# A fused attention and feed-forward kernel: the hand-kept order of all five queues and of the PSUM banks is replaced by another

## The chip, the cores and the metric

The kernel runs on one core of a Trainium2 chip. The metric is the device time of one execution in microseconds (us); lower is better. The core has a matrix engine (TensorE; PE in the profile, its weight loads PEld), a vector engine (VectorE, DVE), a scalar engine (ScalarE, ACT), a general engine (GpSimd, POOL) and a queue that only issues transfers (SyncE, SP). Each runs its instructions in the order in which the program lists them, and waits at an instruction until the semaphores that it names are reached.

## The reference

```python
P = sort_net                                  # 4 batches x 8 heads x 8 x 8
for _ in range(5):                            # "Sinkhorn": normalize rows, then columns
    P = exp(P - max(P, -1)); P = P / (sum(P, -1) + 1e-9); P = P / (sum(P, -2) + 1e-9)
k_sorted = einsum('bhij,bhjcd->bhicd', P, k in 8 blocks of 96 rows)    # the same for v
scores = (q_block @ k_sorted_block.T) / 8     # block by block: 96 x 96
attn = softmax(scores);  o = attn @ v_sorted_block
x = o as 3072 tokens x 512                    # batch x sequence, heads side by side
h = x @ w_in                                  # 512 -> 2048
g = max(h, 0) + alpha * min(h, 0)
out = g @ w_out                               # 2048 -> 512
```

q, k and v are 4 x 8 x 768 x 64 and the result 3072 x 512, all float32; the kernel multiplies in bf16.

## The kernel before, in words

The 4 batches of 8 blocks make 32 steps, g = 0 to 31 (batch b = g // 8). A step handles one block of 96 tokens for all 8 heads. What stands here with a line number is line 1 to 1141 of the kernel before; the changed file is one line shorter from the ORDER table on, so that its lines are lower by one.

**Sinkhorn** (lines 546 to 560) is one chain of small instructions on DVE, with one exponential of ACT in each of its five rounds; its last product is `Pb`. PE spreads `Pb` over the partitions (line 570 for batch 0, lines 593 and 597 for the others), and DVE makes the mixing matrices of it: `BDQ` for the keys of batch 0, `BDM` for those of the others, `BDV` for the values.

**Preparation of a batch.** `k` and `v` are loaded by POOL's queue into `KS` and `VST` (two buffers each). For batches 1 to 3 `conv_k` (L659, POOL) and `conv_v` (copies by L399, on POOL, ACT or DVE) lay them out with zeros between; `prep_k` (L671) and `prep_v` (L700) are PE's products with the mixing matrices, and ACT or DVE copies the results to `KT` and `VS`. `q` of batch 0 is transposed by PE (`prep_q`, L631). For the other batches it goes into `QN`, one load for each of 8 heads (L432), and `turn_q` (L442) turns it from `QN` into `QT` by six transposing DMAs on SP, each of which waits for all eight heads.

**A step of attention.** Scores on PE (L740 for batch 0, L737 for the others), the maxima on DVE (L747), the exponential on ACT (L791, L779), the product with `VS` on PE (L802), reciprocal and scaling to `xq` on DVE (L807, L810), and the transposed result in `xT`. In batch 0 the exponential is made on transposed scores, which PE computes a second time (L759) and from which it subtracts the maxima (L771). In the others the exponentials `Esb` are transposed to `ET` by a DMA on SP (L784). `xq` becomes `xT` by PE (L824) and a copy in batches 0 and 1, by a transposing DMA (L817) in batches 2 and 3.

**Feed-forward.** `ffn1` (L845) multiplies `xT` by `w_in` in pieces of 192 or 384 tokens, ACT takes the relu of the negative into `t` (L852), DVE makes `hT` (L856). The first six tiles of 128 tokens are multiplied by `w_out` in the plain way (`ffn2`, L879). The rest goes in pairs, with seven products in place of eight (`ffn2_pair`, products at L939); their sums and differences (L932, and L904 for the weights) run on DVE or POOL, the results are copied or added into `outstg` (L399, L950) and stored by SP (L890, L981).

**What sets the order.** The code above records 1268 operations and what each reads and writes. Two tables then decide all: `ORDER` lists for each of the five queues which operation comes after which (so it also decides whether ACT or DVE, or DVE or POOL, does an operation that either can do), and `BANKS` gives each product its PSUM bank of the eight. An entry with a dot in PE's list, `24.0`, is not an operation but so many idle products of the identity by itself into that bank (L1101). The code derives the semaphores and waits from these tables:

```python
                if e == "pe" and op.ten is not None and op.ten.ops[0] is op:
                    starts.append(op.ten)
...
        for t in starts:
            for b in t.b:
                if holds[b] is not None:
                    t.ops[0].deps.update(x.idx for x in holds[b].ops)
                holds[b] = t
```

## Time and profile before

| | |
|---|---|
| median of 3 runs | 233.16 us (230.76, 233.16 and 234.16) |
| the profiled execution | 231.25 us, its span 229.5 us |
| outside the span | 1.75 us |
| busy in the span | PE 218.8, PEld 158.2, DVE 188.2, ACT 155.0, POOL 143.0 us |
| moved | 29.01 MB, 126 GB/s |

The span runs from the first instruction of the profiled execution to the last. Matrix products overlap each other, and the profile models their ends, so a busy PE says that work is in flight, not that it runs at its peak. Rows of a timeline give the start in the span, the duration, engine, line, operation and tiles; in brackets stands the idle time of the engine ahead of it and what ended it. Times below are those of the profiled execution, counted from the start of its span.

### The profile page before, as it was taken

What the parts mean: (1) busy time and instruction counts of PE and PEld (TensorE: products, weight loads), DVE (VectorE), ACT (ScalarE), POOL (GpSimd) and SP (SyncE); (2) the same over time, 40 slices, a digit from 0 to 9 for tenths busy, and PEclk for the clock granted to TensorE, in tenths of its full rate; (3) what the DMA queues carried; (4) which work ended last, traced back from release to release, by engine and by line L of the source; (5) the groups of instructions that cost most, each with busy time, mean ns of one, the idle gap of its engine ahead of it and who ended that gap; (6) DMA issues with size and microseconds to landing.
All of it is one profiled execution on the core that took longest, in us unless ns stands there. A gap on an engine that the chain in (4) does not pass through costs nothing.

```text
span 229.5 us, 6469 instructions
## 1 busy us (share of the span) xinstructions
PE 218.8 (95%) x2581; PEld 158.2 (69%) x2581; DVE 188.2 (82%) x393; ACT 155.0 (68%) x428; POOL 143.0 (62%) x159
## 2 busy tenths in 40 slices
PE   2989989899999999999999999999999999999995
PEld 2367868787556655756568786787767777666884
DVE  4757899996879978998999988988799977758942
ACT  4335876867898877898887898679876424456220
POOL 7992929669598999999999499437000312095030
PEclk9999999999999999999999999999999999999999
DMA  5999999999769999989995462765624404200115
GB/s 88 192 208 192 212 206 200 197 109 164 143 113 109 227 141 131 152 159 199 138 93 98 86 160 64 99 146 65 148 60 106 97 20 97 85 27 0 72 68 183
DMA packets 64718, 29.01 MB, mean 126 GB/s; under 512 B 55328, under 2 KB 60464, under 8 KB 64688
## 3 DMA queue, kind: packets, MB, share of 16 engines
q0 software_dynamic: 25216, 13.63, 46.6%
q1 hardware_dynamic: 39472, 14.97, 34.3%
q8 instruction: 20, 0.33, 0.6%
q14 instruction: 10, 0.08, 0.1%
HBM read 27.28 MB, written 6.29 MB: 146 GB/s over the span
## 4 chain that ended last, share of the span: by engine, by line
PE 80%; DVE 13%; ACT 3%; POOL 2%; issue 1%; POOLq 0%
PE ps L845 31%; PE ps L939 23%; PE ps L879 9%; PE ps L700 4%; DVE hT L856 3%; PE ps L802 3%; PE ps L737 3%; DVE xq L810 2%; PE ps L671 2%; DVE nm L747 2%; DVE VDz L399 1%; ACT t L852 1%; PE ps L824 1%; DVE SS L932 1%; PE ps L1101 1%
## 5 line engine op out<-in xcount | busy, mean ns | idle before, releaser
L845 PE MATMUL ps<-xT,w_in_bf 128*128 128x384 bf16 (+1 forms) x576 | 96.2, 308 | 0.1
L856 DVE SCALAR_TENSOR_TENSOR hT<-t,omaT,ps 128x384 bf16<-128x384 f32 (+1 forms) x144 | 75.4, 561 | 11.6 <-ACT t L852 11.1
L852 ACT ACTIVATE t<-ps 128x384 f32<-128x384 f32 x128 | 59.1, 494 | 32.1 <-PE ps L845 19.7
L845 PEld LDWEIGHTS ps<-xT,w_in_bf 128*128 128x128 bf16 x576 | 51.0, 98 | 24.7 <-DVE hT L856 0.8
L779 ACT ACTIVATE Esb<-ps,nf 96x96 bf16<-96x96 f32 x192 | 46.2, 354 | 3.2 <-DVE nf L747 3.1
L399 POOL COPY VDz<-VST 64x384 bf16<-64x384 bf16 x40 | 35.0, 875 | 12.4 <-PE ps L700 5.6
L939 PE MATMUL ps<-w_out_bf,hT 128*128 128x256 bf16 x288 | 35.6, 273 | 0.0
L939 PEld LDWEIGHTS ps<-w_out_bf,hT 128*128 128x128 bf16 x288 | 27.6, 98 | 4.2
L659 POOL COPY KSz<-KS 64x512 bf16<-64x512 bf16 x36 | 23.4, 651 | 8.8 <-DMA KS<-in_k_dram 3.9
L747 DVE TENSOR_REDUCE nf<-ps 96x8 f32<-96x768 f32 x24 | 22.6, 949 | 3.9 <-PE ps L737 3.8
L879 PE MATMUL ps<-w_out_bf,hT 128*128 128x512 bf16 x96 | 24.0, 379 | 0.0
L932 POOL TENSOR_TENSOR hT<-hT,SS 128x1024 bf16<-128x1024 bf16 x6 | 12.7, 2124 | 18.1 <-PE ps L939 16.5
L810 DVE TENSOR_TENSOR xq<-ps,rec 96x512 bf16<-96x512 f32 x32 | 21.9, 684 | 0.9
L399 ACT ACTIVATE outstg<-ps 128x256 f32<-128x256 f32 (+1 forms) x28 | 11.6, 419 | 15.1 <-PE ps L939 13.3
L432 POOL DMA_DIRECT2D QN<-in_q_dram x24 | 19.9, 845 | 0.5 <-DMA QT<-QN 0.5
L399 ACT ACTIVATE VS<-ps 112x512 bf16<-112x512 f32 (+1 forms) x24 | 16.3, 689 | 5.2 <-PE ps L700 5.0
L939 PE MATMUL ps<-TS,SS 128*128 128x256 bf16 x144 | 18.5, 272 | 0.5 <-DVE SS L932 0.5
L932 POOL TENSOR_TENSOR SS<-SS,hT 128x1024 bf16<-128x1024 bf16 x3 | 6.4, 2123 | 20.0 <-DVE SS L932 19.9
L932 POOL TENSOR_TENSOR SS<-hT 128x1024 bf16<-128x1024 bf16 x3 | 6.4, 2122 | 16.6 <-DVE hT L856 16.6
L950 DVE TENSOR_TENSOR outstg<-outstg,ps 128x256 f32<-128x256 f32 x27 | 11.1, 413 | 6.8 <-PE ps L939 5.1
L939 PEld LDWEIGHTS ps<-TS,SS 128*128 128x128 bf16 x144 | 13.8, 98 | 3.1 <-issue 0.8
L802 PEld LDWEIGHTS ps<-VS,ET 112*128 112x128 bf16 (+1 forms) x256 | 11.5, 98 | 3.2 <-DVE VS L399 0.6
(113 smaller groups left out, 290.3 us busy)
## 6 DMA issues: line engine op xcount, KB each, us to landing
out_dram<-outstg SPq DMA_DIRECT2D x22, 256.0 KB, 2.5
KS<-in_k_dram POOLq DMA_DIRECT2D x3, 768.0 KB, 10.6
QN<-in_q_dram POOLq DMA_DIRECT2D x24, 96.0 KB, 7.1
w_in_bf<-in_moe_w_in_dram POOLq DMA_DIRECT2D x4, 512.0 KB, 15.3
w_out_bf<-in_moe_w_out_dram POOLq DMA_DIRECT2D x2, 1024.0 KB, 19.5
VST<-in_v_dram POOLq DMA_DIRECT2D x4, 384.0 KB, 9.1
hT<-in_v_dram POOLq DMA_DIRECT2D x2, 384.0 KB, 8.4
hT<-in_q_dram POOLq DMA_DIRECT2D x1, 768.0 KB, 7.3
```

The costliest lines, as they stand in the source:

```text
L399: return e.activation(o, i, ACTF.Copy) if e is nc.scalar else e.tensor_copy(o, i)
L432: G.add(POOL, lambda e, h=h: e.dma_start(AP(QN, h % 4 * 128 + (h // 4) * 64, [[3072, 128], [512, 6], [1, 64]]), AP(q.tensor, b * HB + h * ...
L659: G.add(POOL, lambda e, hp=hp: e.tensor_copy(AP(KSz, hp * 64 * 3072 + u % 3 * 1024 + hp * 64, [[3072, 64], [128, 8], [1, 64]]), AP(KS[n], ...
L747: G.add(DVE, lambda e: e.tensor_reduce(AP(nx, 0, [[8, 96], [4, 2], [1, 4]]), AP(ps, X.at(), [[LP, 96], [X.step, 2], [96, 4], [1, 96]]), Ax ...
L779: inst = e.activation(AP(Esb[me], p * 128, [[1024, 96], [64, 2], [1, 48]]), AP(ps, X.at((p % 4) * 96) + p // 4 * X.step, [[LP, 96], [48, 2 ...
L810: G.add(DVE, lambda e: e.tensor_tensor(out=AP(xq[me], 0, [[512, 96], [256, 2], [64, 4], [1, 64]]), in0=AP(ps, Z.at(), [[LP, 96], [Z.step, ...
L845: inst = e.matmul(AP(ps, T.at(x * n), [[LP, 128], [1, n]]), AP(w_in_bf, kt * DFF + ft * 128, [[KT_TILES * DFF, 128], [1, 128]]), AP(xT, kt ...
L852: G.add(ACT, lambda e: e.activation(AP(t1[tb], 0, [[384, 128], [1, w]]), AP(ps, T.at(), [[LP, 128], [1, w]]), ACTF.Relu, scale=-1.0), t_ac ...
L856: G.add(DVE, lambda e, x=x, ft=ft: e.scalar_tensor_tensor(out=AP(hT, ft * RING + tok % RING, [[FT_TILES * RING, 128], [1, n]]), in0=AP(t1[ ...
L879: inst = e.matmul(AP(ps, T.at(), [[LP, 128], [1, n]]), AP(hT, ft * RING + tok % RING, [[FT_TILES * RING, 128], [1, 128]]), AP(w_out_bf, ft ...
L932: G.add(VECTOR, lambda e: e.tensor_tensor(out=out, in0=a, in1=b, op=op), {"dve": 690, "pool": 2450}, r=r, w=w, prio=prio)
L939: inst = e.matmul(AP(ps, T.at(), [[LP, 128], [1, 256]]), AP(a.tensor, a.offset + k * a.ap[1][0], [a.ap[0], a.ap[2]]), AP(w.tensor, w.offse ...
```

## The change

Only the two tables are replaced. No operation is added or taken away, and no duration, size or buffer changes, save for two things that the tables themselves hold: the idle products are 12 + 4 + 2 in place of 24 + 1 + 4 + 2, and operations that two engines can do change sides. ACT has 248 operations in its list in place of 259, DVE 401 in place of 393, POOL 158 in place of 155. The new order is said to come from a search with a model in which program fetches and loads in flight hold transposing DMAs back. The diff, cut to the start of three lists (the numbers are the operations in the order in which the code records them):

```diff
     "pool": """
-        7 12 9 4 5 6 11 17 134 19 133 31 118 127 15 116 117 18 124 16 119 285 120 126 287 128 121 315 130 32 236
+        6 31 9 4 5 7 12 18 16 17 133 19 11 134 124 117 32 15 116 128 126 120 235 287 236 118 119 130 131 315 229
...
     "sync": """
-        0 1 169 170 171 387 174 172 173 433 403 463 256 342 375 493 529 535 393 594 499 565 439 409 561 469 645
+        1 0 169 170 171 173 174 172 387 403 256 433 463 342 493 499 409 529 439 393 594 565 535 469 632 561 375
...
     "pe": """
-        3 24.0 155 78 1.2 84 96 94 122 82 92 86 98 90 88 114 104 108 4.2 145 110 2.6 147 135 112 148 102 193 137
+        3 12.0 122 82 78 84 90 98 92 86 94 96 88 108 110 102 155 4.3 104 112 145 135 2.1 114 147 148 193 137 138
```

**PE, the first products.** What PE does between the burst of small products that opens the program (`bz`) and the scores of the first steps. Before:

```order
L1101 MATMUL ps<-identb 128x512 x24
L593 MATMUL ps<-Pb,selk 128x64
L597 MATMUL ps<-Pb,selk 64x64 x2
L570 MATMUL ps<-Pb,w_out_bf 128x8 x24
L1101 MATMUL ps<-identb 128x512
L631 MATMUL ps<-identb,hT 64x128 x16
L647 MATMUL ps<-BDQ,KS 64x128 x16
L1020 MATMUL ps<-identf,alphaR 128x16
L631 MATMUL ps<-identb,hT 64x128 x16
L647 MATMUL ps<-BDQ,KS 64x128 x8
L631 MATMUL ps<-identb,hT 64x128 x16
L647 MATMUL ps<-BDQ,KS 64x128 x24
```

And in the changed kernel:

```order
L1100 MATMUL ps<-identb 128x512 x12
L1019 MATMUL ps<-identf,alphaR 128x16
L630 MATMUL ps<-identb,hT 64x128 x16
L569 MATMUL ps<-Pb,w_out_bf 128x8 x24
L630 MATMUL ps<-identb,hT 64x128 x16
L646 MATMUL ps<-BDQ,KS 64x128 x24
L630 MATMUL ps<-identb,hT 64x128 x16
L646 MATMUL ps<-BDQ,KS 64x128 x24
L699 MATMUL ps<-BDV,hT 128x64 x24
L592 MATMUL ps<-Pb,selk 128x64
L596 MATMUL ps<-Pb,selk 64x64 x2
```

One of the three transposes of `q` and the transpose of `alpha` now stand ahead of the first product that needs `Pb`, twelve idle products and a further single one are gone, and the spreading of `Pb` for batch 1 comes later.

**DVE, the first maxima.** The same stretch on DVE, from the second of two writes of `BDQ` to the maxima of the first steps. Before:

```order
L399 CAST KT<-ps 128x128x4 x2
L399 COPY QT<-ps 128x128x8
L399 CAST VS<-ps 96x64x8
L607 TENSOR_REDUCE dsel<-outstg 128x16
L747 TENSOR_REDUCE nm<-ps 96x8
L1023 TENSOR_SCALAR omaT<-ps 128x16
L612 TENSOR_TENSOR BDM<-mkhM,dsel 128x64
L747 TENSOR_REDUCE nm<-ps 96x8
L399 CAST VS<-ps 96x64x8
L747 TENSOR_REDUCE nm<-ps 96x8 x2
```

And in the changed kernel:

```order
L398 COPY QT<-ps 128x128x8
L398 CAST KT<-ps 128x128x4
L398 COPY QT<-ps 128x128x8
L398 CAST KT<-ps 128x128x4 x2
L398 COPY VDz<-VST 64x8x48
L746 TENSOR_REDUCE nm<-ps 96x8 x2
L601 TENSOR_TENSOR outstg<-ps,mkj 128x64
L601 TENSOR_TENSOR outstg<-ps,mkjV 128x64
L398 COPY VDz<-VST 64x8x48
L498 MEMSET ET 128x16
L746 TENSOR_REDUCE nm<-ps 96x8 x2
```

DVE now does two copies of `QT` and two `conv_v` copies into `VDz` in this stretch, and one cast to `VS` less; one of the `VDz` copies stands right ahead of the first maximum.

**POOL, the last loads of `QN` for batch 1.** POOL's queue from its last loads of `QN` to the loads for batch 2 (`KS0`, `VST0`). Before, from the last four heads on:

```order
L432 DMA QN<-in_q_dram 128x6x64 x2
L659 COPY KSz<-KS1 64x8x64
L432 DMA QN<-in_q_dram 128x6x64
L659 COPY KSz<-KS1 64x8x64
L432 DMA QN<-in_q_dram 128x6x64
L659 COPY KSz<-KS1 64x8x64
L904 TENSOR_TENSOR TS0<-w_out_bf 128x1024
L399 COPY VDz<-VST1 64x8x48
L659 COPY KSz<-KS1 64x8x64
L399 COPY VDz<-VST1 64x8x48
L659 COPY KSz<-KS1 64x8x64
L469 DMA VST0<-in_v_dram 64x3072 x2
```

And in the changed kernel, from the last two heads on:

```order
L431 DMA QN<-in_q_dram 128x6x64
L658 COPY KSz<-KS1 64x8x64
L1014 DMA w_out_bf<-in_moe_w_out_dram 128x8x512
L658 COPY KSz<-KS1 64x8x64 x2
L457 DMA KS0<-in_k_dram 128x3072
L658 COPY KSz<-KS1 64x8x64
L431 DMA QN<-in_q_dram 128x6x64
L468 DMA VST0<-in_v_dram 64x3072
L398 COPY VDz<-VST1 64x8x48
L658 COPY KSz<-KS1 64x8x64
L903 TENSOR_TENSOR TS0<-w_out_bf 128x1024
L398 COPY VDz<-VST1 64x8x48 x2
```

The second half of `w_out` and all of `k` for batch 2 are now loaded ahead of the last head of `QN`; both stood elsewhere before (the former ahead of the last five heads, the latter behind both loads of `VST0`). On SP all six `turn_q` of batch 1 now stand ahead of the first `ET` transpose, where three stood before it and three behind.

## The prediction, made blind

> **What bounds the kernel now.** I read the head of the page and the chain of work that ended last, then a table by stage, then what PE waits for.

> ```profile
> span 229.5 us, 6469 instructions
> PE 218.8 (95%) x2581; PEld 158.2 (69%) x2581; DVE 188.2 (82%) x393; ACT 155.0 (68%) x428; POOL 143.0 (62%) x159
> PEclk9999999999999999999999999999999999999999
> PE 80%; DVE 13%; ACT 3%; POOL 2%; issue 1%; POOLq 0%
> ```

> PE is busy 95% of the span, at the full clock in every slice, and makes 80% of the chain; DVE follows with 13%. The table by stage shows where that holds (window and its length; busy time of PE, PEld, DVE, ACT, POOL; PE's clock; mean DMA share; GB/s):

> ```profile
> 13.50:36.84 23.34, 21.97 (x436) 18.53 (x437) 18.32 (x39) 15.81 (x24) 14.91 (x20) 1.00 1.18 204
> 13.50:44.00 30.50, 28.21 (x554) 24.27 (x555) 25.10 (x51) 21.56 (x34) 21.33 (x27) 1.00 1.25 202
> 44.00:60.00 16.00, 16.00 (x212) 12.55 (x214) 13.14 (x38) 12.39 (x26) 11.28 (x15) 1.00 1.32 133
> 60.00:130.00 70.00, 69.23 (x739) 44.24 (x734) 62.99 (x114) 59.27 (x188) 62.75 (x76) 1.00 1.14 141
> 130.00:226.80 96.80, 96.78 (x925) 73.19 (x923) 78.66 (x151) 56.67 (x168) 35.59 (x22) 1.00 0.37 87
> ```

> From 13.5 us on PE is without work in flight for 30.50 - 28.21 = 2.29 us up to 44, nothing up to 60, 0.77 up to 130 and 0.02 after that: 3.08 in all. Since no product is added or taken away, an order can win these 3.1 us and what the start holds, and hardly more. The waits say what the 3.1 us are (who waits, for whom: us, times, longest):

> ```profile
> PE ps L824 <- DVE xq L810: 1.5, 3, 0.9
> PE ps L593 <- DVE Pb L560: 0.6, 1, 0.6
> PE ps L802 <- DVE VS L399: 0.5, 1, 0.5
> PE ps L939 <- DVE SS L932: 0.5, 1, 0.5
> PEld ps L845 <- DVE hT L856: 0.8, 3, 0.4
> ```

> The first three lie ahead of 44 us, the last two behind it. All name DVE. None names a transposing DMA: the transfers that the new order is said to care for are not what PE waits for now.

> **The change, part by part.** *1. The start.* Rows of the timeline (start, duration, engine, line, operation):

> ```profile
> 9.08 0.15 PEld L1101 LDWEIGHTS ps<-identb 128*128 128x128 bf16 x1 [0.28 <-issue]
> 9.51 2.94 PEld L1101 LDWEIGHTS ps<-identb 128*128 128x128 bf16 x14 [0.28 <-issue]
> 13.57 0.20 PE L593 MATMUL ps<-Pb,selk 32*128 32x64 bf16 x1 [0.62 <-DVE Pb L560]
> 14.57 0.39 PE L1101 MATMUL ps<-identb 128*128 128x512 bf16 x1
> 14.89 0.64 PE L631 MATMUL ps<-identb,hT 128*64 128x128 bf16 x16
> 15.91 0.23 PE L1020 MATMUL ps<-identf,alphaR 16*128 16x16 f32 x1
> 16.07 0.64 PE L631 MATMUL ps<-identb,hT 128*64 128x128 bf16 x16
> 16.54 0.39 PE L647 MATMUL ps<-BDQ,KS 128*64 128x128 bf16 x8
> ```

> `Pb` is made by DVE's Sinkhorn chain, which stays as it is, so I leave its time at 13.5. PE then finds already done what now stands ahead of it: the transpose of `alpha` (16.07 - 15.91 = 0.16) and one `prep_q` (16.54 - 16.07 = 0.47); the single idle product (14.89 - 14.57 = 0.32) is gone. That is 0.95 us less behind `Pb`. The twelve idle products taken away cost nothing while PE waits for `Pb` anyway.

> By the last 14 weight loads, 2.94 / 14 = 0.21 us apart, PE is already at its faster pace well before `Pb`; the one ahead of them came 0.43 before. [...]

> *2. DVE up to 44 us.* What it is given, and what leaves it:

> ```profile
> 18.84 1.22 DVE L399 COPY QT<-ps 128x1024 bf16<-128x1024 bf16 x1
> 19.97 0.68 DVE L399 CAST VS<-ps 96x512 bf16<-96x512 f32 x1
> L399 DVE COPY VDz<-VST x3: 558/927/2079, 27.3 to 48.3; 64x384 bf16<-64x384 bf16 x3
> 36.84 0.95 DVE L747 TENSOR_REDUCE nm<-ps 96x8 bf16<-96x768 f32 x1
> 40.91 2.08 DVE L399 COPY VDz<-VST 64x384 bf16<-64x384 bf16 x1
> 43.99 0.34 PE L824 MATMUL ps<-identb,xq 96*128 96x96 bf16 x4 [0.92 <-DVE xq L810]
> ```

> Ahead of the last maximum of batch 0 (before at 36.84) come one more copy of `QT` (1.22) and two copies into `VDz` (2 x 0.93), 3.1 us; small additions of some 1.1 (two sorts, `mkjV`'s product and a copy of `xT`) and two casts to `VS` less (2 x 0.68 = 1.4) leave **+2.8 us**. DVE is idle 23.34 - 18.32 = 5.0 us of that stretch, but not where the work is added: the extra `QT` copy and a `VDz` copy stand ahead of the first two maxima, which score products wait for. Walked down DVE's list with these durations, the last maximum comes some 0.9 us later than before, counted from the start of the span, and PE has up to 2.0 us of new waits by then. Against that, the 2.08 us copy at 40.91, which made the 0.92 us wait at 43.99, is no longer in front of that product. 2.0 - 1.0 = **+1.0**, and with the start **0** at 44 us. The ends: if the added copies all fall into idle time, -2; if all of the 2.8 us stay and the old wait stays too, +2.

> *3. Weights and `q` of batch 1.* The loads of POOL's queue come one behind the other.

> ```profile
> 49.25 1.10 POOL L469 DMA_DIRECT2D VST<-in_v_dram  x2
> 50.90 4.85 SPq L442 DMA_TRANSPOSE QT<-QN  x3
> 59.73 0.56 PE L737 MATMUL ps<-KT,QT 64*96 64x96 bf16 x16
> QT<-QN SPq DMA_TRANSPOSE x3, 7.0
> QT<-QN SPq DMA_TRANSPOSE x2, 2.5
> KS<-in_k_dram POOLq DMA_DIRECT2D x3, 768.0 KB, 10.6
> VST<-in_v_dram POOLq DMA_DIRECT2D x4, 384.0 KB, 9.1
> w_out_bf<-in_moe_w_out_dram POOLq DMA_DIRECT2D x2, 1024.0 KB, 19.5
> q0 software_dynamic: 105, 0.55, 101.1%
> DMA to landing us min/median/max: 14.1/15.3/18.8
> ```

> (The two rows with the three and the two transposes are those issued in 50.5 to 53.9 and in 64.3 to 67; the row of q0 is the only queue with packets in the former stretch; the last row is `w_in`'s.) Before, the last head of `QN` landed when SP could issue, at 50.90. In the new order all of `k` for batch 2 (768 KB) lies ahead of it: at 202 GB/s 786 / 202 = 3.9 us, so **54.8**. The transposes issued at 50.90 took 7.0 us and no packet of theirs moved while POOL's loads did; the same kind took 2.5 with the loads gone. The two halves of `VST` stand directly behind the last head, 393 / 202 = 1.9 us each, so loads run until about 58.6; 2.5 on makes **61.1** for the first tile. PE came to its scores at 59.73 before, and the work listed ahead of them is 0.4 us more. Held back, the scores wait 61.1 - 60.1 = 1.0; slipping in between the two halves, they wait for nothing. I take **+0.8**, near the first, since the row with 7.0 is the nearest one; by these two ends the term lies between 0 and the 6.0 of the first rival.

> [...]

> The second half of `w_in` now lies behind half of `w_out`: 1024 KB and a head more, about 5.7 us. It was there at 16.48 + 18.8 = 35.3 before, so about 41; its first reader stands where PE comes at 41 to 43. Price 0, at most 1.5.

> *4. From 44 us to the last product.* The two waits behind 44 us hold 1.3 us. Added up with the durations that PE's rows have before, more PE work stands in the new list between a step's `o` and the first product of the feed-forward that reads it: for g = 15 9.8 us in place of 6.0, for g = 18 8.2 in place of 5.2, for g = 30 8.8 in place of 4.6. Tighter are g = 23 (5.2 for 7.3) and, between scores and `o`, g = 31 (7.0 for 12.9). I take half of the waits: **-0.7**; ends -1.3 and, if the tighter ones each cost a wait of the kind now seen, +1. That POOL has two more large sums at 2.1 us and ACT less costs nothing, as both idle a quarter of the time or more.

> *5. The end* (last products, copy, store) is the same: **0**.

> Sum: 0 + 0.8 - 0.7 = +0.1 on the profiled execution, 231.25 us, so 231.35. That execution lies 1.9 under the median of 233.16 (its runs lie between 230.76 and 234.16), and a new median can fall anywhere between; I forecast **232.2**.

> **The rivals.** *Loads push the transposes out (slower).* `VST`'s second half stands behind a `w_out` sum of 2.1 us and copies that wait for PE. If POOL issues it only at about 54.5, with its median of 9.1 to landing, loads end at 63.6 and the first tile comes at 66.1: 6.0 us of waiting in place of 0.8, 231.35 + 5.2 = **236.6** by the profiled execution, 238.5 by the median. From a landing at 60.1 on each us counts in full, as all products behind the scores in PE's list wait with them. For it: a DMA share of 1.32 in the stage and the 7.0 us row. Against: 49.25's halves needed only some 5 to 7. 0.14 with all its milder forms beyond 3 us.

> *DVE becomes the bound.* If the two added `VDz` copies take 2.08 us as that at 40.91 did, and not 0.93 (it lay beside a sum on POOL), DVE has 2 x 1.15 = 2.3 us more in a stretch in which PE follows it: 231.35 + 2.3 = 233.7, and with the upper end of step 2 in place of its 0, **235.7**. 0.10.

> *A colder PE.* If twelve idle products no longer bring PE to its faster pace, the products behind `Pb` go at half the pace until as much work is done as the twelve that are missing were, 12 x 0.21 = 2.5 us at most: 231.35 + 2.5 = **234**, by the median 236. 0.05.

> *All waits go.* The start's 0.95, PE's idle of 2.29 without the 0.6 for `Pb`, which stays, and the 0.8 behind 60 us: 231.25 - 3.4 = **227.8**, the floor for any order. For it: each wait names DVE, and copies are moved in front of it. Against: the added 2.8 us on DVE. 0.11.

> *The change does nothing that is seen*, since no wait named a transposing DMA: this is the forecast's own neighbourhood, **231 to 233**.

> **How the numbers follow.** The forecast has 0.60 (229.5 to 234.5), the rivals 0.14, 0.10, 0.05 and 0.11. For 8 in 10 the range takes the forecast's own, the colder PE, DVE as bound and the nearer halves of the two outer cases: **228.5 to 236.5**. About 2%, 4.7 us, is what a measurement of this kernel can tell from no change; faster than 228.5 is the floor alone, 0.10; slower than 237.8 is the far part of the loads' case with a little of DVE's, 0.11; the rest 0.79.

> **What would show it.** Step 1: the last `prep_k0` of batch 0 about 1 us earlier against `Pb`. Step 2: the last maximum of batch 0 near 37.8 and no wait near 0.9 for `xq`. Step 3: the first transposes of `q` issued near 54.8, landed near 61, and a wait of the scores L736 for `QT`. Step 4: fewer waits for `hT` and `SS`. The prediction is wrong if PE's idle time from 13.5 on is over 6 us or under 1, or if PE's weight loads ahead of `Pb` are still 0.42 apart.

## The result, and the profile after

The changed kernel takes **242.4 us** (median of 4 runs, 241.35 to 242.71) against 233.4 of the kernel before: a ratio of 1.040 (95% interval 1.031 to 1.049). Slower by 4%, outside the range, on the side that I had given 0.11. Here and below a ratio leaves out runs more than 1.5% above the fastest of the same kernel. The profiled execution, 242.55 us, has a span of 240.8. The head of its page, with the lines that answer to those shown of before:

```profile
span 240.8 us, 6443 instructions
PE 223.1 (93%) x2568; PEld 162.0 (67%) x2568; DVE 193.6 (80%) x401; ACT 150.5 (63%) x417; POOL 151.4 (63%) x162
PEclk9977995799999999999999999999999999999999
PE 64%; DMA 10%; DVE 9%; POOL 9%; ACT 4%; issue 2%; POOLq 0%; ACTq 0%
```

The third line is what I had not looked for: PE's clock is not full in the third and fourth slice nor in the seventh and eighth. Before, it was full in every slice. And PE's share of the chain has fallen from 80% to 64%, with 10% for DMA, which was not named before, and 9% for POOL, which had 2%. The table by stage, cut at the places where the clock changes (columns as before: after POOL's come clock, DMA share and GB/s):

```profile
11.30:14.70 3.40, 2.46 (x59) 1.78 (x57) 2.10 (x13) 1.02 (x3) 3.34 (x6) 1.00 1.12 223
14.70:21.50 6.80, 4.83 (x79) 4.69 (x79) 3.43 (x5) 2.00 (x3) 3.43 (x5) 0.50 1.05 215
31.80:35.20 3.40, 2.46 (x53) 1.73 (x50) 3.22 (x7) 2.58 (x5) 3.17 (x6) 1.00 1.24 207
35.20:45.40 10.20, 9.97 (x123) 8.49 (x122) 9.33 (x18) 3.78 (x6) 4.10 (x4) 0.50 1.18 134
60.00:130.00 70.00, 66.14 (x701) 40.36 (x700) 60.37 (x109) 55.24 (x167) 60.98 (x73) 1.00 1.00 133
130.00:226.80 96.80, 95.55 (x930) 70.95 (x929) 80.16 (x152) 62.93 (x190) 44.08 (x31) 1.00 0.45 88
```

PE has half its clock from 14.7 to 21.5 us and from 35.2 to 45.4, 17 us in all. Each time a stretch of 3.4 us goes ahead in which it was busy for 2.46 us. Before, it was busy for longer in the same two stretches:

```profile
11.30:14.70 3.40, 2.77 (x36) 1.54 (x34) 1.70 (x9) 0.35 (x2) 3.40 (x5) 1.00 1.10 217
31.80:35.20 3.40, 3.00 (x71) 2.32 (x66) 3.33 (x7) 3.19 (x6) 2.23 (x4) 1.00 1.23 206
```

Beyond 60 us the clock is full, and PE still lacks 3.9 us up to 130 (before 0.77) and 1.25 up to 226.8 (before 0.02). What PE waits for, from its waits (who, for whom: us, times, longest):

```profile
PE ps L646 <- DMA KS<-in_k_dram: 2.1, 1, 2.1
PE ps L670 <- POOL KSz L658: 1.2, 1, 1.2
PE ps L844 <- DVE xT L398: 1.2, 1, 1.2
PE ps L699 <- POOL VDz L398: 1.0, 1, 1.0
PE ps L823 <- DVE xq L809: 0.7, 1, 0.7
PE ps L938 <- DVE outstg L398: 0.7, 1, 0.7
PE ps L736 <- DMA QT<-QN: 0.5, 1, 0.5
```

Before, all waits from 13.5 us on named DVE; now loads, transposes and POOL's copies stand there. The timeline shows where each comes from:

```profile
16.67 1.49 PE L646 MATMUL ps<-BDQ,KS 128*64 128x128 bf16 x24 [2.08 <-DMA KS<-in_k_dram]
32.92 0.34 PE L823 MATMUL ps<-identb,xq 96*128 96x96 bf16 x4 [0.68 <-DVE xq L809]
37.20 2.12 POOL L903 TENSOR_TENSOR TS<-w_out_bf 128x1024 bf16<-128x1024 bf16 x1 [0.81 <-DMA w_out_bf<-in_moe_w_out_dram]
37.38 2.31 DVE L398 COPY VDz<-VST 64x384 bf16<-64x384 bf16 x1
45.70 0.84 POOL L398 COPY VDz<-VST 64x384 bf16<-64x384 bf16 x1 [5.52 <-PE ps L699]
61.13 2.12 POOL L903 TENSOR_TENSOR TS<-w_out_bf,TS 128x1024 bf16<-128x1024 bf16 x1
61.23 2.10 DVE L617 TENSOR_TENSOR BDV<-mkhV,dsel 128x64 bf16<-128x64 f32 x1
110.28 0.83 POOL L431 DMA_DIRECT2D QN<-in_q_dram  x1 [3.06 <-ACT t L851]
118.40 0.39 PE L699 MATMUL ps<-BDV,VDz 128*128 128x64 bf16 x8 [0.96 <-POOL VDz L398]
```

`KS` of batch 0 comes late (16.5 us, before 14.5), and PE stands for 2.08 us. Twice a DVE operation that takes 0.2 to 0.9 us elsewhere takes over 2, each time beside one of POOL's sums of 2.12. POOL stands 5.5 us at a copy that needs a product of the slowed PE, and the loads of `QN`, `w_out` and `KS` queued behind it go out late. At 107 us it stands 3.1 us at a load of `QN`; the profile names ACT there, but the transposing DMA that still read `QN`, issued at 105.5, landed 4.2 us later, at 109.7, just ahead.

Two theories for the first 60 us stood against each other: **C**, the clock is the loss, as PE starves and is slowed for it; and **O**, the new order's own waits are, and the clock only shows them. For the rest: **L**, the late part has waits of its own, or **K**, they only follow from the delay.

### The profile page after: what moved, and what is told of

Its sections match the earlier page's. It is cut to its first block, busy times and chain, and to the rows that moved or that the text cites. A ratio compares the mean times of both kernels' runs of the same rounds, so it can differ in the third digit from the quotient of the medians.

```text
span 240.8 us, 6443 instructions
## 1 busy us (share of the span) xinstructions
PE 223.1 (93%) x2568; PEld 162.0 (67%) x2568; DVE 193.6 (80%) x401; ACT 150.5 (63%) x417; POOL 151.4 (63%) x162
## 4 chain that ended last, share of the span: by engine, by line
PE 64%; DMA 10%; DVE 9%; POOL 9%; ACT 4%; issue 2%; POOLq 0%; ACTq 0%
PE ps L844 25%; PE ps L938 19%; DMA KS<-in_k_dram 5%; PE ps L878 4%; PE ps L699 4%; DMA ET<-Esb 3%; ACT Esb L778 3%; PE ps L801 3%; POOL VDz L398 3%; DVE hT L855 3%; POOL hT L931 2%; PE ps L736 2%; POOL QN L431 2%; DMA out_dram<-outstg 2%; DVE xq L809 2%
## 5 line engine op out<-in xcount | busy, mean ns | idle before, releaser
L855 DVE SCALAR_TENSOR_TENSOR hT<-t,omaT,ps 128x384 bf16<-128x384 f32 (+1 forms) x144 | 76.1, 562 | 16.5 <-ACT t L851 16.0
L844 PEld LDWEIGHTS ps<-xT,w_in_bf 128*128 128x128 bf16 x576 | 52.0, 99 | 24.4 <-DVE xT L398 1.3
L931 POOL TENSOR_TENSOR hT<-hT,SS 128x1024 bf16<-128x1024 bf16 x7 | 15.2, 2172 | 27.7 <-PE ps L938 27.5
L658 POOL COPY KSz<-KS 64x512 bf16<-64x512 bf16 x36 | 23.5, 653 | 11.4 <-DMA KS<-in_k_dram 7.7
L938 PEld LDWEIGHTS ps<-w_out_bf,hT 128*128 128x128 bf16 x288 | 27.3, 98 | 4.6 <-DVE xq L809 0.3
L878 PE MATMUL ps<-w_out_bf,hT 128*128 128x512 bf16 x96 | 23.2, 379 | 0.0
L398 ACT ACTIVATE outstg<-ps 128x256 f32<-128x256 f32 (+1 forms) x24 | 10.0, 416 | 19.6 <-PE ps L938 19.5
L398 ACT ACTIVATE VS<-ps 112x512 bf16<-112x512 f32 (+1 forms) x23 | 15.8, 693 | 8.0 <-PE ps L699 7.8
L931 POOL TENSOR_TENSOR SS<-hT 128x1024 bf16<-128x1024 bf16 x2 | 4.2, 2124 | 17.3 <-DVE hT L855 17.2
L801 PEld LDWEIGHTS ps<-VS,ET 112*128 112x128 bf16 (+1 forms) x256 | 11.6, 101 | 4.5 <-ACT Esb L778 0.9
L878 PEld LDWEIGHTS ps<-w_out_bf,hT 128*128 128x128 bf16 x96 | 8.6, 98 | 8.4
L801 PE MATMUL ps<-VS,ET 112*128 112x65 bf16 (+1 forms) x256 | 13.6, 199 | 0.6 <-DMA ET<-Esb 0.3
## 6 DMA issues: line engine op xcount, KB each, us to landing
KS<-in_k_dram POOLq DMA_DIRECT2D x3, 768.0 KB, 13.3
w_out_bf<-in_moe_w_out_dram POOLq DMA_DIRECT2D x2, 1024.0 KB, 15.2
VST<-in_v_dram POOLq DMA_DIRECT2D x4, 384.0 KB, 10.5
hT<-in_v_dram POOLq DMA_DIRECT2D x2, 384.0 KB, 9.8
hT<-in_q_dram POOLq DMA_DIRECT2D x1, 768.0 KB, 9.3
```

What stands on the lines that cost most here:

```text
L398: return e.activation(o, i, ACTF.Copy) if e is nc.scalar else e.tensor_copy(o, i)
L658: G.add(POOL, lambda e, hp=hp: e.tensor_copy(AP(KSz, hp * 64 * 3072 + u % 3 * 1024 + hp * 64, [[3072, 64], [128, 8], [1, 64]]), AP(KS[n], ...
L801: inst = e.matmul(AP(ps, Z.at(h4 * 68) + hp * Z.step, [[LP, 128], [1, 65]]), AP(ET[et], pos(h4, hp) * 96, [[800, nk], [1, 128]]), AP(VS[n] ...
L844: inst = e.matmul(AP(ps, T.at(x * n), [[LP, 128], [1, n]]), AP(w_in_bf, kt * DFF + ft * 128, [[KT_TILES * DFF, 128], [1, 128]]), AP(xT, kt ...
L855: G.add(DVE, lambda e, x=x, ft=ft: e.scalar_tensor_tensor(out=AP(hT, ft * RING + tok % RING, [[FT_TILES * RING, 128], [1, n]]), in0=AP(t1[ ...
L878: inst = e.matmul(AP(ps, T.at(), [[LP, 128], [1, n]]), AP(hT, ft * RING + tok % RING, [[FT_TILES * RING, 128], [1, 128]]), AP(w_out_bf, ft ...
```

## The experiments

The diffs show the place in a queue's list where the edit lies; the numbers are the operations. Where runs of one kernel scatter, they stand with the mean clock of the run.

**1. Idle products into the wait for `KS`** (`90` is the first `prep_k0`; `8.4` eight idle products into bank 4).

```diff
 changed kernel, pe:
-        3 12.0 122 82 78 84 90 98 92 86
+        3 12.0 122 82 78 84 8.4 90 98 92 86
```

> The changed kernel with eight idle products put into PE's 2.08 us wait for `KS` (ahead of the first `prep_k0`); nothing else differs. Theory C (the clock): PE runs at half clock from 14.7 to 21.6 us because it stood idle there, and again from 35.2 to 45.4; with the wait filled, the first cold stretch is gone and prep_k0 takes 0.23 us a group in place of 0.43, so the time falls by 1.2 us at least, to about 241, and to 237 if the second cold stretch goes with it. Theory O (the order's own waits on DVE and POOL; the clock only shows that PE waits): the idle products fill a wait and change nothing, 242.4 +- 1.

Measured 240.97 (clock 0.979), 236.03 (0.999), 240.71 (0.986) and 240.72 (0.964). The one run in which the clock stayed full is 4.7 us faster than the median: theory C, by one run. Why it fell in the others shows in the timeline of the profiled one:

```profile
13.21 0.80 PE L569 MATMUL ps<-Pb,w_out_bf 32*128 32x8 bf16 x24 [1.01 <-DVE Pb L559]
14.93 3.10 PE L1100 MATMUL ps<-identb 128*128 128x512 bf16 x8
```

The eight idle products are already at the slow pace, 3.10 / 8 = 0.39 us each: PE had been short of work ahead of `Pb`, where twelve idle products are missing.

**2. The kernel before with the new start of PE.**

```diff
 kernel before, pe:
-        3 24.0 155 78 1.2 84 96 94 122 82 92 86
+        3 12.0 122 82 155 78 84 96 94 92 86
```

> The kernel before with only PE's start of the changed kernel: 12 idle products in place of 24, the single one taken out, the transpose of alpha and one prep_q ahead of Pb. Theory C: `KS` is there at 14.5 us, PE has no long wait, the clock stays full and the start is worth 0.5 to 1 us: 232.5 to 233 against 233.4. Rival W (twelve idle products are too few to warm PE): the clock is down for a stretch near 13 to 20 us and the kernel takes 1 to 3 us longer, 234.5 to 236.5.

233.31 us, median of ten (clock 0.971 to 0.992), ratio 1.0075 (1.0038 to 1.0113). Against the median of the kernel before beside it, 232.2, the step that I had priced at -0.95 costs 1.1 us: the mechanism of rival W (half clock from 14.0 to 17.4 us and again from 31.1 to 41.3 in the profiled run), at less than the price that it gave.

**3. The kernel before with 12 idle products, and nothing else.**

```diff
 kernel before, pe:
-        3 24.0 155 78 1.2 84
+        3 12.0 155 78 1.2 84
```

> The kernel before with 12 idle products at the start in place of 24, nothing else changed: PE has nothing from about 10.8 us to `Pb` at 13.6. Theory C: PE goes to half clock near 14 us, and the kernel takes 1 to 3 us longer than before (234 to 236 against 232.3). Rival N: the idle products ahead of `Pb` do nothing and the time is unchanged within 0.5.

233.59 us, median of ten, ratio 1.0056 (1.0018 to 1.0094); the clock is 0.985 in nine runs and 0.991 in one, and in the profiled one it is half from 13.6 to 20.4. That is 1.5 us over the median of 232.1 beside it, and nothing else was changed. So the idle products were not idle: they held the clock.

**4 and 5. The new order to 70 us, then the old; and the old to 46 us, then the new.** Each queue's list is one kernel's up to the operations started by then, and the other's behind it.

```diff
 changed kernel, pe, at the seam:
-        338 339 460 430 340 370 371 421 540
+        338 339 340 430 370 451 371 460 421
```

> The changed kernel's order for all that it starts in its first 70 us, then the order of before. Up to 70 us the changed kernel has fallen 8.1 us behind; behind it another 3.4 us more than the kernel before. Theory L (the late part of the new order has waits of its own): 242.4 - 3.4 = 239. Rival K (the waits behind 70 us only follow from the delay ahead of it): about 242.

> The order of before for all that it starts in its first 46 us, then the changed kernel's order. Theory L: the waits that the changed kernel has behind 46 us come again, 5.4 us more than before's: 238 to 239. Rival K (they follow from the late start): 232 to 234, with the clock full throughout.

The first: 239.82 us, and 235.57 in the one run with a full clock. By that run 4.3 us of the early part are the clock; 235.6 - 231.0 = 4.6 are left at full clock. Against the 242.4 of the changed kernel the old order behind 70 us saves 2.6, near the 3.4 of theory L. The second gave 243.8 (ratio 1.045, 1.036 to 1.054), which neither theory had, and decides nothing: loads of the two orders are mixed at its seam, and its profile has waits of 2.8 and 2.7 us at 47 and 53 us that neither kernel has.

**6. A cleaner seam: the old order to 100 us, then the new.**

```diff
 kernel before, pe, at the seam:
-        582 671 598 588 636 566 585 624 720
+        582 671 598 566 585 624 588 569 720
```

> The order of before for all that it starts in its first 100 us, then the changed kernel's order: a place where no load of the one order is left behind one of the other. Theory L (the late part has waits of its own: for VDz 1.0 at 118.4, for KSz 1.2 at 138.1, for outstg 0.7 at 231.8): 3 us over before, 234 to 236. Rival K (they follow from the delay): 231.5 to 233.

234.4 us (233.97 to 238.67, the clock 0.991 to 0.993 in each run), ratio 1.0115 (1.0063 to 1.0166). That is the time of theory L, but not its mechanism: the profiled run, 233.97, has no wait for `VDz`, `KSz` or `outstg` behind the seam. What PE loses stands at the seam itself, a wait and a slow stretch behind it:

```profile
101.86 3.80 PE L845 MATMUL ps<-xT,w_in_bf 128*128 128x384 bf16 x12 [1.22 <-DVE hT L856]
101.99:105.40 3.41, 3.41 (x12) 1.65 (x11) 1.18 (x2) 0.86 (x4) 3.32 (x5) 0.50 1.03 91
```

From 106 to 226 us PE is without work for 0.6 us, as before. So by this trace the new order loses nothing there behind the old one, and the late waits of the changed kernel come from it together with what its own first part leaves behind; experiments 11 and 12 show how. No trace shows what the run of 238.67 met.

**7. A warm start for the changed kernel.**

```diff
 changed kernel, pe:
-        3 12.0 122 82 78 84 90 98
+        3 18.0 122 82 78 84 8.4 90 98
```

> The changed kernel with 18 idle products at the start in place of 12 and eight more ahead of the first prep_k0, so that PE has work nearly all the time from 6.5 us on. Theory C (the clock): the runs of the former kernels lie near 236 where the clock was full and near 240.5 where it was 0.97 to 0.98, so with a warm start the clock is at 0.99 or above and the time 235.5 to 237. Rival O: the clock falls later all the same (PE waits for DVE at 32 to 40 us) and the time stays at 240 to 242.5.

241.49 us, clock 0.972 to 0.979. The first slow stretch is gone, the clock full until 33.2; then it is half until 46.9. Rival O came true for the time: two waits of PE for DVE's `xq`, 0.68 and 0.42 us, lie in the 3.4 us ahead of the fall at 33.2.

**8. POOL's sums away from DVE's copies** (`658` and `659` are sums).

```diff
 changed kernel, pool:
-        231 319 132 658 230 359 125
+        231 319 132 230 658 359 125
...
-        355 368 239 659 323 543
+        355 368 239 323 659 543
```

> The changed kernel with two of POOL's 2.12 us sums (L903) moved one and two operations later in POOL's list, so that they do not start beside DVE's copy into `VDz` (2.31 us at 37.38 where others take 0.6 to 0.9) and beside DVE's product for `BDV` (2.10 at 61.23 where another takes 0.4). Theory P (POOL's sum holds the DVE operation until it ends): both take their short time, PE's waits near 36 to 40 us and the 1.2 us wait for `xT` at 63.6 go, 2 to 3 us less: 239.5 to 240.5. Rival: the two are slow for themselves, no change, 242.4.

In DVE's timeline the same operations are short:

```profile
36.35 0.62 DVE L398 COPY VDz<-VST 64x384 bf16<-64x384 bf16 x1
57.45 0.87 DVE L617 TENSOR_TENSOR BDV<-mkhV,dsel 128x64 bf16<-128x64 f32 x1
```

0.62 in place of 2.31, 0.87 in place of 2.10: theory P for the operations, and the second slow stretch is missing in the profiled run (236.70 us, clock 0.985). The others took 241.34 (0.972), 243.91 (0.986) and 240.16 (0.979), so a gain in time isn't clear. The wait for `xT` is gone; the scores of step 8 now wait 1.9 us for the first tiles of `QT` instead. In the changed kernel both operations had ended just behind the sum of 2.12 us (39.69 against 39.32 us, 63.33 against 63.25), as theory P has it; by what means a sum holds them is not shown.

**9. The loads of `QN` for batch 1 first** (`125` and `129` are loads, `121` is half of `w_out`, `359` the copy that waits for PE).

```diff
 changed kernel, pool:
-        658 230 359 125 276 121 280 279 369 275 129 367
+        658 230 125 129 121 359 276 280 279 369 275 367
```

> The changed kernel with POOL's last two loads of QN and the second half of w_out moved ahead of the copy into VDz that waits 5.5 us for PE (issued near 40 us in place of 46.5 to 51.3). Theory Q (the transposes of q wait for their loads): the last head lands near 50 in place of 63.9, the first tile of QT by 58, the scores of step 8 do not wait (0.74 us less), and the rest of the way is unchanged: 241 to 242. Theory C alone would leave 242.4, since the clock falls before that.

242.29 (clock 0.979), 240.04 (0.957), 246.16 (0.929) and 246.63 (0.965): no gain that these runs can show. The last head landed at 44.9 in place of 63.9 and step 8 did not wait, but the transposes landed far later than the 2.5 us that two of them took in the kernel before while only their own queue had packets (64.3 to 67 us). Those issued from 46.3 to 48.5 and from 48.6 to 50.5 (landing in us), and the row of POOL's queue for the former stretch:

```profile
QT<-QN SPq DMA_TRANSPOSE x2, 7.5
QT<-QN SPq DMA_TRANSPOSE x2, 11.6
q0 software_dynamic: 351, 0.36, 114.5%
```

What moved while the first two waited were, beside one program fetch, packets of POOL's queue alone (the row of q0); `w_out` was in flight until 52.1, `KS` until 57.9. That is only the start of it. From 48.9 us on the transposes' queue (q1) has packets too, and between 53 and 58 us, while POOL's loads run, the two queues move nearly as many packets:

```profile
q0 software_dynamic: 154, 0.84, 95.2%
q1 hardware_dynamic: 137, 0.03, 5.0%
```

So the transposes first stood for 4 us, for a reason that no run here tests, and then moved beside the loads, slowly all the same: a packet of theirs is some 0.2 KB and one of the loads 5.5 KB, so that 137 packets brought them 0.03 MB and 154 brought the loads 0.84.

**10. The three mends together.**

```diff
 changed kernel, pe and pool:
-        3 12.0 122 82 78 84 90 98
+        3 18.0 122 82 78 84 8.4 90 98
-        132 658 230 359 125 276 121 280 279 369 275 129 367
+        132 230 658 125 129 121 359 276 280 279 369 275 367
-        355 368 239 659 323 543
+        355 368 239 323 659 543
```

> The changed kernel with the three edits together: 18 idle products at the start and eight ahead of prep_k0, POOL's two sums moved off DVE's copies, the loads of QN ahead of the waiting copy. If theories C, P and Q name the causes ahead of 70 us, the clock is at 0.985 or more and what is left is DVE's added work (about 2 us) and the late waits (about 3): 235 to 237. If the second cold stretch near 33 to 46 us comes all the same, 239 to 241.

238.07 (clock 0.978), 242.85, 242.68 and 241.07 (0.993 each). The clock no longer explains the time: at 0.993 no more than one stretch of 3.4 us can have been slow (half the clock for 3.4 of 240 us lowers the mean by 0.007), and these runs are still at 241 to 243. Something else takes the gain back. No trace shows one of these three runs; that of experiment 9 had POOL standing 5.6 us at a load of `QN` near 104 to 110.

**11. Copies ahead of the loads of `QN` for batch 3** (`619`, `617`, `616` are loads; `682` to `681` copies into `VDz`).

```diff
 changed kernel, pool:
-        615 683 614 619 682 617 685 613 620 729 684 681 622
+        615 683 614 682 685 613 620 729 684 681 619 617 622
...
-        867 616 734 843 871 733
+        867 843 871 616 734 733
```

> The changed kernel with three loads of QN for batch 3 moved behind copies on POOL's list: two that stand at 110.3 and 111.9 us go behind five copies into VDz, one at 134.9 behind the copies into KSz. Theory H (a load of QN must wait until the transposing DMAs have read QN; they are held back by other loads, and the copies queued behind the load wait with it, then PE): POOL's 3.1 us wait moves behind the copies, PE's waits for VDz at 118.4 (1.0) and for KSz at 138.1 (1.2) go, 2 to 3 us less than 242.4: 239.5 to 240.5. Rival: POOL is late at these places for its own work; no change.

238.10 (0.978), 233.62 (0.999), 241.03 (0.979), 239.97 (0.956). PE's waits for `VDz` at 118 and for `KSz` at 138 are gone: theory H. The time scatters with the clock; the run at full clock, 233.62, is 2.3 to 2.4 us under those of experiments 1 (236.03) and 12 (235.96). Of POOL's waits for the transposes this is left there:

```profile
POOL QN L431 <- DMA QT<-QN: 0.5, 1, 0.5
```

**12. POOL's first operations as before.**

```diff
 changed kernel, pool:
-        6 31 9 4 5 7 12 18 16 17 133 19 11 134 124
+        7 12 9 4 5 6 11 17 134 19 133 31 18 16 124
```

> The changed kernel with POOL's first twelve operations in before's order (the loads of v for batch 1 at 7.1 and 8.5 us in place of 9.3 and 11.3). Theory S (the order of these operations makes `KS` of batch 0 land at 16.1 to 16.5 us in place of 14.0 to 15.5): it lands by 15.5, PE's 2.08 us wait is under 1 us, and the first cold stretch is shorter or gone: 240 to 241.5. Rival: `KS` lands at 16 all the same, and its time varies from run to run.

`KS` landed at 14.5 us: theory S. Over all profiled kernels it came at 14.0 to 15.5 with the old first operations (9 kernels) and at 15.3 to 16.5 with the new (9). Which of these operations does it was not tried. The clock stayed full to 118 us, and PE came to the scores of step 8 at 61.7, in the changed kernel at 67.8 (this kernel's row first):

```profile
61.73 0.38 PE L736 MATMUL ps<-KT,QT 64*96 64x96 bf16 x8 [0.42 <-DMA QT<-QN]
67.80 0.38 PE L736 MATMUL ps<-KT,QT 64*96 64x96 bf16 x8
```

And yet three runs took 241.0 to 242.5, the profiled one 242.49 (one took 235.96, clock 1.0). Most of the 6 us gained are given back at one place, as the waits of POOL between 95 and 142 us and those of PE show:

```profile
POOL QN L431 <- DMA QT<-QN: 6.1, 1, 6.1
PE ps L699 <- POOL VDz L398: 3.8, 1, 3.8
```

PE comes to this wait 4.5 us sooner than in the changed kernel (112.9 against 117.4), but the load of `QN` that waits for the transposes goes out only 1.4 us sooner (108.86 against 110.28). Behind PE's wait the clock is half from 118.1 to 121.5.

**13. Edits 7, 8, 9 and 11 together.**

```diff
 changed kernel, the lines of 10 and in pool:
-        615 683 614 619 682 617 685 613 620 729 684 681 622
+        615 683 614 682 685 613 620 729 684 681 619 617 622
-        867 616 734 843 871 733
+        867 843 871 616 734 733
```

> The changed kernel with the edits of the run with three mends (idle products, sums off the copies, loads of QN for batch 1) and those on the loads of QN for batch 3 together. If the causes add, the run with three mends (238 to 242.8) loses its late waits (1.55, 0.6 and 1.3 us) and most of its spread: 235 to 237.5. If POOL's wait for the transposes only comes at another place, 238 to 242.

240.5 us, ratio 1.034 (1.022 to 1.046). The clock is full to 75 us, and then PE waits 2.4 us for `KSz` at 74. The copies into `KSz` stand on POOL's list behind one that waits for a load of `VST`:

```profile
67.42 2.70 POOL L398 COPY VDz<-VST 64x384 bf16<-64x384 bf16 x3 [5.25 <-DMA VST<-in_v_dram]
```

That load took 11.9 us from issue to landing, in experiment 10, which has the same edit 9, 6.2. Why it was late here isn't shown. The mends don't simply add up.

**14 and 15. Edits 11 and 12; and with edit 8 as well.**

```diff
 changed kernel, pool, the lines of 11 and:
-        6 31 9 4 5 7 12 18 16 17 133 19 11 134 124
+        7 12 9 4 5 6 11 17 134 19 133 31 18 16 124
 in the second kernel also:
-        231 319 132 658 230 359 125
+        231 319 132 230 658 359 125
-        355 368 239 659 323 543
+        355 368 239 323 659 543
```

> The changed kernel with both edits: POOL's first twelve operations as before (KS landed at 14.5 us with it, and the clock stayed full to 118 us), and the copies ahead of the loads of QN for batch 3 (with it PE's waits for VDz and KSz near 118 and 138 us were gone). If these two are the causes of the loss, the clock is at 0.99 or more and what stays is the wait for xT near 57 to 63 us (1.3), that for the first tiles of QT (0.9 to 1.6) and the one for outstg near 230 (0.9): 233 to 234.5 in most runs. If something further is missing, 236 or more.

> The same with POOL's two sums moved off DVE's copies as well. Theory P: the 1.3 us for xT go. If the transposes of q are then what is late, as their loads hold them back, the scores of step 8 wait for them instead (1.9 us in the run that had only this edit) and the time is the same, 233 to 234.5; if not, 232 to 233.

The first: 239.97 (0.971), 235.65, 232.06 and 235.44 (1.0 each); these three differ by 3.6 us at one clock, so the clock is not the only thing that varies from run to run, and what else does is open. The second: **235.0 us**, 234.91 to 236.50, clock 0.992 to 1.0, ratio 1.018 (1.0105 to 1.0255). Three edits of POOL's list, with the banks and all other lists as in the changed kernel, take back 7.4 of the 10 us, and the runs lie within 1.6 us. It is 0.5 us over what I had expected at most, and with edit 8 it isn't clearly faster than without (232.06 to 235.65 at full clock). What PE still waits for:

```profile
PE ps L736 <- DMA QT<-QN: 1.4, 2, 1.2
PE ps L823 <- DVE xq L809: 1.4, 3, 0.7
PE ps L938 <- DVE outstg L398: 1.1, 1, 1.1
```

**16. The kernel before, warm and with its own sum moved** (`657` is the sum at 40.49).

```diff
 kernel before, pe and pool:
-        3 24.0 155 78
+        3 26.0 155 78
...  pe: 2.4 ahead of 140, 3.2 ahead of 313
-        232 132 235 657 323 230 355
+        232 132 235 323 230 657 355
```

> The kernel before with two more idle products ahead of `Pb`, two ahead of the first product with `VS` and three ahead of the transpose of step 6 at 43.99, and POOL's sum at 40.49 moved behind the next two copies, away from DVE's copy at 40.91. Theories C and P: the clock stays at 1.0 in every run and the 0.92 us wait goes, so the time is 229.5 to 230.5 against a median of 232.2 to 233.4. Rival: the idle products only push real ones back, 232 to 234.

**230.68 us**, median of twelve runs, 230.27 to 231.26, ratio 0.9958 (0.9932 to 0.9984): the fastest median of all kernels here, 0.2 us above the range that I had given, and the clock is 1.0 in every run. The copy that took 2.08 us is short, and POOL's sum starts behind it:

```profile
41.11 0.92 DVE L399 COPY VDz<-VST 64x384 bf16<-64x384 bf16 x1
42.59 2.13 POOL L904 TENSOR_TENSOR TS<-w_out_bf 128x1024 bf16<-128x1024 bf16 x1
```

It also explains the scatter of the kernel before. Of 57 runs of it beside the experiments, the 24 with a clock of 0.999 or 1.0 have a median of 231.0 us, the 25 from 0.991 to 0.998 one of 232.6, the 8 below 0.98 one of 234.7. With the clock held, only the 231 remain. The idle products and the moved sum were not tried apart; since 231.0 is what the kernel before takes at full clock, the moved sum can be worth some 0.3 us at most.

## Why the prediction was wrong

*What bounds the kernel* was right as far as it went: PE, and its waits. But I took the full clock of one profiled execution for a property of the order. The runs of before that took 232.5 and 234.7 were ones in which it fell.

*Step 1, the start: the step that failed first.* Forecast -0.95, "the twelve idle products taken away cost nothing while PE waits for `Pb` anyway"; no run had shown that. Experiments 2 and 3 measure +1.1 and +1.5 us by the medians of all runs (+0.75% and +0.56% by the ratios). My rival "a colder PE" had the slow clock, but as a start that is too short to warm PE, and gave it 0.05. The sign that I had named for it came: the weight loads of all twelve are still 0.43 us apart, and the other sign, over 6 us of idle time from 13.5 us on, came as well (3.25 + 3.86 + 1.25 = 8.4).

```profile
10.27 0.15 PEld L1100 LDWEIGHTS ps<-identb 128*128 128x128 bf16 x1 [0.28 <-issue]
10.70 0.15 PEld L1100 LDWEIGHTS ps<-identb 128*128 128x128 bf16 x1 [0.28 <-issue]
```

Yet they did warm PE: the clock was full from 11.3. What I didn't ask is what stands behind them: a stretch of 3.4 us in which PE was busy for 2.46 was enough to lose the clock again. No long gap was needed: the longest in the stretch ahead of 14.7 us was 0.48 us, and that ahead of 35.2 was 0.68. Every slow stretch in these traces that ended within the span lasted 3.4 us or a multiple of it (6.8 and 10.2 in the changed kernel, 13.7 in experiment 7), and of one kernel's runs some had one and others none (experiment 1: clock 0.964 to 0.986 in three runs, 0.999 in the fourth). The second half of the step's error: I left `KS` at 14.5 us, since its load stands at the same place among the loads. It came at 16.5.

*Step 2, DVE up to 44 us.* Forecast +1.0, ends -2 and +2. With a full clock and `KS` on time (experiment 12) PE reaches step 8 at 61.7 against 59.73, 2.0 us late, of which 0.42 is the wait for `QT`: near the upper end of steps 1 and 2. That one of the added copies would take 2 us beside a sum was my second rival; it came so, and a product for `BDV` with it. With the slow clock PE came to step 8 only at 67.8.

*Step 3, the transposes of `q`.* Forecast: last head at 54.8, first tile at 61.1, a wait of 0.8. Measured 63.9, 67.8 and 0.5; in experiments 8, 12 and 15, which have it less late, the wait is 1.3 to 1.9. That the transposes land late while loads run was right, and experiment 9 shows it harder than before (11.6 us against 7.0). But I took from the row of q0 that they can't move at all; experiment 9 shows more than that, 4 us without a packet of theirs and then nearly as many packets of the one queue as of the other. What I missed is that POOL's loads were themselves behind a copy that waits for PE.

*Step 4, 44 us to the last product.* Forecast -0.7, by counting how much PE work lies between a step's products. I counted PE's list and not POOL's. There the new order puts loads of `QN`, each of which must wait until the transposes have read the tile, ahead of copies that PE needs. With the changed kernel's first 70 us the old order behind them saves 2.6 us (experiment 4), and PE waits 3.8 us at one such place in experiment 12; copies moved ahead of the loads end these waits (experiment 11). With the old order's first 100 us the same lists cost nothing that the trace shows (experiment 6). So the term isn't a price of the late order alone: it is what that order loses when the transposes ahead of it are late.

*The sum.* Of 242.4 - 231.0 = 11.4 us against the kernel before at full clock, experiment 4 gives 2.6 to the late part, 4.3 to the clock and 4.6 to the early part at full clock. The split rests on one run with a full clock; experiment 1 has 4.7 for the clock, by one run as well. In the changed kernel's profile the wait for `KS` is 2.1 and that for `xT` 1.2. These parts overlap, since a later wait swallows an earlier one. 235.0 - 232.3 = 2.7 us of experiment 15 stay. No run changes the bank table by itself, so its part in them isn't shown.

## What to carry to other kernels

Where the clock of an engine falls behind a stretch of little work, as PE's did here behind 2.46 us in 3.4, idle time ahead of the critical stretch has a price of its own: before taking idle products out, look at the work that each stretch of that length gives the engine, not only at its busy time, and at the clock of all runs, not of one profile. In a queue that works in order, look for each instruction that must wait for a slow transfer and ask what stands behind it; a gain ahead of such a place can be lost there. And keep a 2 us sum of POOL from starting beside DVE's short copies, which it made 2 us long here (2.31 us beside a sum, 0.62 with the sum moved).

## What the runs showed of the hardware

```profile
28.10:31.50 3.40, 2.31 (x56) 1.93 (x54) 2.71 (x8) 3.02 (x4) 3.29 (x5) 1.00 1.65 189
```

So the share of busy time alone doesn't decide it. Once slow, PE stayed so for one to four lengths of 3.41 us, in the changed kernel for 10.2 us of which it was busy 9.97.

Weighed by work, both come into line. Give each product the time that its columns take at the pace of the idle products (0.21 us for 512 in the profile of before), times the size of its weights as a share of 128 x 128, and divide each trace into the lengths of 3.41 us at whose ends its clock changes. In the 18 traces that makes 1139 lengths up to 225 us. Of the 34 with work for 0.34 of their time or less, 32 had half clock behind them; of the 1076 with more than 0.39, none; of the 29 between, 11. The two ahead of the falls in the changed kernel held 0.26 and 0.29, that of experiment 15 above 0.37, and the two behind which the changed kernel stayed slow after 35.2 us held 0.35 and 0.30 although PE was busy nearly all the time: most of its products there have smaller weights (from 35.2 to 42 us all but 8 of 84, 64 x 96 and 96 x 128 among them). The lowest of the kernel before's profile up to 225 us, 0.39 at 26.6, lies at the edge, which fits a clock that falls in some of its runs. An idle product has weights of 128 x 128, and so counts in full. This sorts the traces; no run here changes the shape of the products alone.

The scatter of the kernel before, 230 to 236 us, went with this clock, and seven idle products with one moved sum took it away.
